# The attention's own-token term as a matrix product through the identity, and a weight subtraction issued half a slot later

## The chip, the cores and the metric

One core of a Trainium2 chip runs the whole program. The metric is the device time of one execution in microseconds (us). The kernel before takes 937.41 us, the median of three runs (937.14 to 937.49).

## The reference

A linear attention with a decaying state, over 4 batches, 8 heads, 768 tokens and 48 channels a head, and then two dense layers with 3072 tokens:

```
for t in range(S):
    cur = einsum('bhd,bhe->bhde', u[None] * k[t], v[t])
    y[t] = einsum('bhd,bhde->bhe', r[t], state + cur)      # cur: the token's own term
    state = w[t][..., None] * state + einsum('bhd,bhe->bhde', k[t], v[t])
x = y as 3072 tokens x 384
x = elu(x @ w_in) @ w_out            # first dense layer, 384 -> 2048 -> 384
x = silu(x @ w_in2) @ w_out2         # second dense layer
```

The token's own term is, for a token and a head, the sum over channels of r*u*k, times the token's value vector v.

## The kernel before, in words

**Units.** The attention is cut into 24 units: 6 stretches of 128 tokens, times 4 batches. For unit n the steps of `prep_steps(n)` run on VectorE (DVE) and ScalarE (ACT): two scans of the decays into the tile `both` (`scan`, `scan_back`), the products r*k (`products`), the scaled r and k (`q`, `kt`, tiles `tq` and `tk`), a range check (`far`, ACT), and for n below SUMMED = 9 the sums of r*u*k for each head on TensorE (PE, `summed`, with u as the moving operand). `diag` then writes, on ACT, the identity matrix times that sum into all eight 128 x 128 blocks of the tile `am` (L201). From unit 9 on GpSimd (POOL) does it in another way (L209). On PE, `pe_steps(n)` makes the scores (`sc`, or `early` for the first four units), DVE copies their strict upper triangle over `am` (`masked`, L312), and `within` multiplies `am` by the values into `y`: 16 matmuls with 32 stationary columns each. So the own term is the diagonal of `am`. `past` (12 such matmuls, L355) adds the state's part, `outer` and `update` renew the state, `split` writes `y` as a rounded part `xh` and the rest `xl`.

**Dense layers.** Tokens go in blocks of four units (512 tokens). A slot is one strip of 128 hidden channels of one block: 9 matmuls into `ph` (`hidden`, L459, three channel groups times the products xh*wh, xl*wh, xh*wl), an activation, a rounding of its result to `gh` (ACT) and `gl` (DVE), and 9 matmuls into `po` for the slot before the last (L490). A block has 16 slots. Here slot s and strip s are numbered from 0, and each of the four units of the next block is spread over the half slots of the present one by `round_ticks`: in block 0 that is units 4 to 7, and the next unit's `prep_steps` run along.

**Weights.** For each strip a load goes to a staging tile `wst` (three buffers, SP queue), ACT scales its halves (`w_scale`, L421, L423), DVE joins them (`w_join`, L430, L432), and `w_split` rounds on ACT (`wh`, L444) and subtracts on DVE (`wl`, L445), whereupon the staging tile is free for the next load. In block 0 the split of strip s+2 is issued in the second half of slot s.

**Order.** The program is recorded under a manual schedule: each engine runs its instructions in the order in which the code issues them, and waits at the head of its own list. `dense_units` writes the order for units 0 to 3, before the first slot; after it come the slots. `behind` is a list of steps that run at the beginning of the next half slot; before, only the last part of `split` goes there.

**Buffers.** `am` has two buffers, `tk` two, `in_w` two. `r*k` (tile `rk`) has a buffer of its own in units 0 to 4 and lies inside `am` after that; `far` writes its unused output into `am`.

Of the kernel before, what the change touches and what calls it, by code (L numbers as in the profile page):

```python
# [34 lines left out]
def kernel(  # L35
# [116 lines left out]
    def prep_steps(n):  # L152
# [32 lines left out]
        def bonus():  # L185
            af = st["af"] = ch_p.tile([128, H * L], F32, tag="am", name="am")
# [7 lines left out]
        def diag(part=0):  # L194
            if n < SUMMED:
                if part == 0:
                    dg = st["dg_sb"] = tok_p.tile([128, H], F32, tag="dg", name="dg")
                    nc.scalar.activation(out=dg, in_=st["dg"], func=ACTF.Copy)
# [4 lines left out]
                return  # L203
            if part:
                return
            dg = tok_p.tile([128, H], F32, tag="dg", name="dg")
            nc.vector.tensor_reduce(
                out=dg, in_=st["kn"].rearrange("p (h d) -> p h d", h=H), axis=mybir.AxisListType.X, op=ALU.add)
            nc.gpsimd.tensor_tensor(  # L209
                out=st["a"].rearrange("p j e t -> p (j e) t"),  # L210
                in0=ident.unsqueeze(1).to_broadcast([128, H, L]),
                in1=dg.unsqueeze(2).to_broadcast([128, H, L]), op=ALU.mult)

        def products():
            if n >= SUMMED:
                return
            if n <= BLOCKS[0]:
                rk = g_p.tile([RB, NP, L], F32, tag="gh", name="rk")
            else:
                rk = st["af"][0:RB, 0:NP * L].rearrange("p (j t) -> p j t", j=NP)  # L220
            st["rk"] = rk
# [24 lines left out]
        def kt():  # L246
            tk = st["kd"] = ch_p.tile([RB, NP, L], F32, tag="tk", name="tk")
# [21 lines left out]
        return dict(ktok=ktok, ktok_copy=ktok_copy, scan=scan, scan_back=scan_back, far=far, whole_decay=whole_decay, bonus=bonus, products=products, summed=summed, diag=diag,  # L269
# [7 lines left out]
    def pe_steps(n, xt, col, free=None):  # L277
# [81 lines left out]
        def within():  # L359
            y = ps["y"]  # L360
            vf = st["v"].rearrange("p j c -> p (j c)")
            for step in range(4):
                for base in range(4):
# [3 lines left out]
                    for kt in range(KT):  # L367
# [8 lines left out]
                        start=not ch and step == 0, stop=step == 3 or todo[step + 1][0] != blk,  # L376
# [59 lines left out]
    def w_split():  # L436
        if whole:
# [7 lines left out]
            nc.vector.tensor_tensor(out=l, in0=t, in1=h.bitcast(F32), op=ALU.subtract)  # L445
# [122 lines left out]
    def round_ticks(n):  # L568
# [9 lines left out]
        def t1():  # L578
# [7 lines left out]
            if n + 1 not in ALONE:  # L586
                load_unit(n + 3, "w")
            pe["masked"](0)

        def t2():  # L590
            pe["masked"](1)
            do("summed")
            do("far")
            do("q")
            do("diag")
# [6 lines left out]
        def t4():  # L602
            do("diag", 1)
            if n < SUMMED - 1:
                do("ktok")
                do("ktok_copy")
# [19 lines left out]
    def dense_units(mask):  # L626
# [19 lines left out]
        for n in range(-1, count):  # L646
# [41 lines left out]
            if more:  # L688
# [5 lines left out]
                p["diag"](0)  # L694
                p["diag"](1)
# [11 lines left out]
        after["kt"]()  # L707
        load_unit(count + 2, "wc")
        after["far"]()
        after["diag"](0)  # L710
        return after
    def prep_rest(at, n, p):

        if n == BLOCKS[0]:
            if at == 1:
                p["diag"](1)
        elif at == 1:
# [5 lines left out]
            load_unit(n + 2, "w")  # L723
        elif at == 2:
# [5 lines left out]
            p["diag"](0)  # L730
            p["diag"](1)
# [42 lines left out]
    with tc.manual_schedule():  # L774
# [11 lines left out]
        first_alone = dense_units(  # L786
# [13 lines left out]
        for j, units in enumerate(BLOCKS):  # L800
# [4 lines left out]
            if ticks and ticks[0] in ALONE:  # L805
                alone = prep_steps(ticks[0]) if j else first_alone

            def tick(part):
# [13 lines left out]
                if j == 0 or final and f % 4 != 3:  # L822
# [19 lines left out]
            assert not todo and not ticks and not behind  # L842
# [195 lines left out]
```

## Time and profile before

| | |
|---|---|
| median of the runs | 937.41 us |
| profiled execution | 938.83 us, of which the span from first to last instruction is 937.1 us |
| PE busy | 919.0 us, 98% of the span |
| DVE, ACT busy | 495.3 us and 501.5 us |
| mean granted PE clock | 0.982 of full speed |

A PE that is busy need not be at its peak, and the granted clock has two levels, 1.2 GHz (shown as 0.50) and 2.4 GHz (1.00). From about 105 us on PE is busy without a pause. Before that it has pauses and stretches at the lower clock, while DVE and ACT are busy most of the time too, and there the three engines wait for each other in turn.

### The profile page before, as it was taken

Reading aid. Unit: us, or ns where it says so; the run is one execution under the profiler, and the core shown is the slowest. Engines: PE = TensorE matmul, PEld = TensorE weight load, DVE = VectorE, ACT = ScalarE, POOL = GpSimd, SP = SyncE. Lnnn points to the kernel's source line nnn. Section 1 sums busy time; section 2 is a strip of 40 time slices with the busy share of each in tenths; the row PEclk is TensorE's granted clock in tenths of the full one; section 3 lists DMA queues with packets and bytes.
Section 4 is the critical chain, followed back from the end, with each engine's and each line's share of the span. In section 5 each row is a group of like instructions: output and inputs, shape, how many; then the busy total and the mean of one; then the engine's idle time right before and its main releaser. Section 6 shows DMA issues by size and latency. Waiting matters only on the chain.

```text
span 937.1 us, 15193 instructions
## 1 busy us (share of the span) xinstructions
PE 919.0 (98%) x6158; PEld 790.0 (84%) x6158; DVE 495.3 (53%) x726; ACT 501.5 (54%) x901; POOL 136.4 (15%) x101
## 2 busy tenths in 40 slices
PE   8899899999999999999999999999999999999997
PEld 7767688888888888888888899999999999899996
DVE  8989988776786776665378852212112222222211
ACT  6798967666555565555488953323333333333322
POOL 0000013463433354442000000000000000000000
PEclk7699999999999999999999999999999999999999
DMA  8655514222221322300245510200200200200001
GB/s 254 156 181 175 167 38 135 67 81 89 82 59 55 102 59 86 97 20 1 102 169 169 176 61 1 68 1 0 69 1 1 68 1 1 68 1 1 34 1 37
DMA packets 32223, 68.69 MB, mean 73 GB/s; under 512 B 3601, under 2 KB 13969, under 8 KB 32145
## 3 DMA queue, kind: packets, MB, share of 16 engines
q1 hardware_dynamic: 32144, 67.64, 23.1%
q8 instruction: 50, 0.82, 0.4%
q14 instruction: 29, 0.23, 0.1%
HBM read 58.19 MB, written 9.44 MB: 72 GB/s over the span
## 4 chain that ended last, share of the span: by engine, by line
PE 91%; DVE 3%; ACT 3%; issue 1%; DVEq 0%
PE ph L459 41%; PE po L498 22%; PE po L490 20%; PE sc L303 2%; PE y L374 2%; PE y L355 2%; ACT am L201 1%; PE ktp L261 1%; PE upd L324 1%; DVE wl L445 1%; DVE am L312 0%; ACT wh L444 0%; PE early L644 0%; DVE wst L430 0%; ACT wst L421 0%
## 5 line engine op out<-in xcount | busy, mean ns | idle before, releaser
L482 DVE TENSOR_TENSOR gl<-g,gh 128x512 fp32r<-128x512 f32 x192 | 146.9, 765 | 317.6 <-ACT gh L481 317.2
L459 PE MATMUL ph<-xh,wl 128*128 128x512 f32 x576 | 227.2, 394 | 2.6 <-DVE wl L445 2.5
L459 PE MATMUL ph<-xh,wh 128*128 128x512 f32 x576 | 227.3, 395 | 1.2 <-ACT wh L444 1.2
L459 PE MATMUL ph<-xl,wh 128*128 128x512 f32 x576 | 226.6, 393 | 0.0
L481 ACT ACTIVATE gh<-g 128x512 fp32r<-128x512 f32 x192 | 120.9, 630 | 145.7 <-PE po L498 109.6
L459 PEld LDWEIGHTS ph<-xh,wl 128*128 128x128 f32 x576 | 108.3, 188 | 28.0 <-DVE wl L445 4.8
L470 ACT ACTIVATE g<-ph 128x512 f32<-128x512 f32 x96 | 57.2, 596 | 138.1 <-PE ph L459 138.1
L498 PE MATMUL po<-wh,gl 128*128 128x384 f32 x384 | 129.5, 337 | 0.0
L498 PE MATMUL po<-wh,gh 128*128 128x384 f32 x384 | 129.3, 337 | 0.0
L498 PE MATMUL po<-wl,gh 128*128 128x384 f32 x384 | 129.0, 336 | 0.0
L459 PEld LDWEIGHTS ph<-xh,wh 128*128 128x128 f32 x576 | 108.5, 188 | 21.7 <-ACT wh L444 1.8
L459 PEld LDWEIGHTS ph<-xl,wh 128*128 128x128 f32 x576 | 108.5, 188 | 19.2
L490 PE MATMUL po<-gh,wh 128*128 128x512 f32 x288 | 114.0, 396 | 0.0
L490 PE MATMUL po<-gl,wh 128*128 128x512 f32 x288 | 112.4, 390 | 0.0
L490 PE MATMUL po<-gh,wl 128*128 128x512 f32 x288 | 112.2, 389 | 0.0
L466 ACT ACTIVATE g<-ph 128x512 f32<-128x512 f32 x96 | 56.8, 592 | 75.7 <-PE ph L459 75.6
L475 DVE SCALAR_TENSOR_TENSOR g<-g,ph 128x512 f32<-128x512 f32 x96 | 65.5, 682 | 43.3 <-ACT g L468 42.3
L498 PEld LDWEIGHTS po<-wh,gh 128*128 128x128 f32 x384 | 72.2, 188 | 4.3
L498 PEld LDWEIGHTS po<-wl,gh 128*128 128x128 f32 x384 | 72.1, 188 | 4.1
L498 PEld LDWEIGHTS po<-wh,gl 128*128 128x128 f32 x384 | 72.0, 188 | 0.0
L237 POOL TENSOR_TENSOR ql<-tq,qh 64x512 fp32r<-64x512 f32 (+1 forms) x30 | 42.6, 1419 | 166.9 <-ACT qh L236 165.8
L490 PEld LDWEIGHTS po<-gh,wh 128*128 128x128 f32 x288 | 54.1, 188 | 11.6 <-issue 0.6
(95 smaller groups left out, 1088.5 us busy)
## 6 DMA issues: line engine op xcount, KB each, us to landing
wst<-in_moe_w_in_dram SPq DMA_DIRECT2D x32, 384.0 KB, 3.3
wst<-in_moe_w_out_dram SPq DMA_DIRECT2D x32, 384.0 KB, 4.4
in_c<-in_rk_ch_dram SPq DMA_DIRECT2D x24, 448.0 KB, 4.3
in_w<-in_w_ch_dram SPq DMA_DIRECT2D x24, 226.2 KB, 2.8
in_v<-in_v_tok_dram SPq DMA_DIRECT2D x24, 224.0 KB, 4.0
x_d<-x2s SPq DMA_DIRECT2D x18, 256.0 KB, 2.5
xl<-x_d SPq DMA_DIRECT2D x6, 768.0 KB, 5.2
out_dram<-os SPq DMA_DIRECT2D x24, 192.0 KB, 2.0
```

Of the source, the lines that this page charges most:

```text
L237: nc.gpsimd.tensor_tensor(out=lo, in0=x, in1=hi.bitcast(F32), op=ALU.subtract)
L303: nc.tensor.matmul(p[:, jj].rearrange("p e t -> p (e t)"), a[:, j, :], b[:, j].rearrange("p e t -> p (e t)"), start=i == 0, stop=i == len( ...
L355: nc.tensor.matmul(y[32 * base:32 * base + 32, kt, :], state[b][:, j, 32 * i:32 * i + 32], st["q"][:, j, :], start=kt == 0, stop=False, sk ...
L374: nc.tensor.matmul(y[32 * base:32 * base + 32, blk // 4, :], vf[:, c:c + 32], st["a"][:, h // 2, h % 2, :], start=not ch and step == 0, st ...
L459: nc.tensor.matmul(ph, lhs, xt[rhs][:, kt, 0:nt], start=n == 0, stop=n == 3 * KT - 1)
L466: nc.scalar.activation(out=g, in_=ph, func=ACTF.Exp)
L470: nc.scalar.activation(out=g, in_=ph, func=ACTF.Silu)
L475: nc.vector.scalar_tensor_tensor(out=g, in0=g, scalar=-1.0, in1=ph, op0=ALU.mult, op1=ALU.max)
L481: nc.scalar.activation(out=gh, in_=g, func=ACTF.Copy)
L482: nc.vector.tensor_tensor(out=gl, in0=g, in1=gh.bitcast(F32), op=ALU.subtract)
L490: nc.tensor.matmul(po[ot][:, 0:nt], lhs, rhs, start=f == 0 and i == 0, stop=f == NF - 1 and i == 2)
L498: nc.tensor.matmul(po[t][:, 0:DM], lhs[:, sl], rhs["o", f], start=f == 0 and i == 0, stop=f == NF - 1 and i == 2)
```

## The change

Five things, all of them for units 0 to 8:

1. `am` is no longer filled with scaled identities. Two fixed tiles `am0`, `am1` are cleared once by POOL; `masked` writes the strict upper triangle, and the rest stays zero.
2. The own term is made by `within`: a tile `vs` holds each token's values times its sum, and 12 matmuls with `vs` stationary and the identity moving add it to `y`, ahead of the 16. `vs` (128 x 384, one buffer) is written by eight ACT operations of 48 columns in units 0 to 4, and by one DVE product in units 5 to 8, one half slot later than before for these.
3. The sums are copied from PSUM by a step of their own, `diag_sums`, ahead of `diag`.
4. `rk` and `tk` are one tile: `kt` overwrites the products in place. `far` writes its unused output into `in_w`, and so the loads of `in_w` stand behind `far`.
5. In block 0 the subtraction `wl` and the next weight load go to `behind`: they are issued at the beginning of the next half slot, behind `gl` of the slot in between.

```diff
+    ams = [one_p.tile([128, H * L], F32, name=f"am{i}") for i in range(2)]
-        for s in state:
+        for s in (*ams, *state):
             nc.gpsimd.memset(s, 0.0)
...
-            to = st["af"][0:RB, 0 if n < SUMMED else H * D:].bitcast(BF16)[:, 0:2 * W1 - 1]
+            to = st["w"].bitcast(BF16)[:, 0:2 * W1 - 1]
...
-                for h in range(part * 4, part * 4 + 4):
-                    nc.scalar.activation(
-                        out=st["a"][:, h // 2, h % 2, :], in_=ident, func=ACTF.Copy, scale=dg[:, h:h + 1])
+                if n > BLOCKS[0]:
+                    nc.vector.tensor_tensor(
+                        out=vs, in0=dg.rearrange("p (j e) -> p j e", e=2).unsqueeze(3).to_broadcast([128, NP, 2, D]),
+                        in1=v3, op=ALU.mult)
+                    return
+                for h in range(H):
+                    nc.scalar.activation(
+                        out=vs[:, h // 2, h % 2, :], in_=v3[:, h // 2, h % 2, :], func=ACTF.Copy, scale=dg[:, h:h + 1])
...
+            rk = st["rk"] = st["kd"] = ch_p.tile([RB, NP, L], F32, tag="tk", name="tk")
             nc.vector.tensor_tensor(out=rk, in0=st["c"][:, 0], in1=st["c"][:, 1], op=ALU.mult)
...
+            if own:
+                vs = st["vs"].rearrange("p j e c -> p (j e c)")
+                for blk in range(KT * 4):
+                    kt, base = divmod(blk, 4)
+                    nc.tensor.matmul(
+                        y[32 * base:32 * base + 32, kt, :], vs[:, 32 * blk:32 * blk + 32], ident,
+                        start=not ch and kt == 0, stop=False, skip_group_check=True)
...
-            nc.vector.tensor_tensor(out=l, in0=t, in1=h.bitcast(F32), op=ALU.subtract)
+            low(lambda: nc.vector.tensor_tensor(out=l, in0=t, in1=h.bitcast(F32), op=ALU.subtract))
...
-                if j == 0 or final and f % 4 != 3:
+                if j == 0 and part:
+                    w_split(behind.append)
+                    behind.append(w_load)
+                elif j == 0 or final and f % 4 != 3:
                     w_tick(part)
```

On PE, among the units before the first slot, unit 0's `within` stands between the transposes of unit 1 (`ktp`) and the sums of unit 2 (`early<-u_ch`). Before:

```order
L295 MATMUL early<-tq,tk 128x128 x8
L261 MATMUL ktp<-ident,tk 128x112 x4
L374 MATMUL y<-am,in_v 32x128 x16
L233 MATMUL early<-u_ch,rk 128x2 x4
L324 MATMUL upd<-in_v,kt 32x48 x3
```

The same place now; the sums read `tk`, which holds the products until `kt` writes it:

```order
L304 MATMUL early<-tq,tk 128x128 x8
L270 MATMUL ktp<-ident,tk 128x112 x4
L376 MATMUL y<-ident,vs 32x128 x12
L391 MATMUL y<-am_101,in_v 32x128 x16
L240 MATMUL early<-u_ch,tk 128x2 x4
L333 MATMUL upd<-in_v,kt 32x48 x3
```

Twelve matmuls came in ahead of the 16, and so ahead of the sums of unit 2.

On DVE, in the same place, unit 2's `tk` (the second row from L248) stands ahead of the first weight join and of unit 1's `masked`; the semaphores that each row waits for stand behind it. Before:

```order
L336 TENSOR_TENSOR packed_105<-upd,whole 112x192 [waits PE_49]
L170 SCALAR_TENSOR_TENSOR both<-in_w,seed 112x515 [waits DVE_49]
L241 TENSOR_TENSOR tq<-in_c,both 112x512
L248 TENSOR_TENSOR tk<-in_c,both 112x512 [waits DVE_49]
L430 SCALAR_TENSOR_TENSOR wst<-wst 128x768 [waits DMAHW4_49,DMAHW3_49,Activation_49]
```

The same place now:

```order
L345 TENSOR_TENSOR packed_107<-upd,whole 112x192 [waits PE_49]
L172 SCALAR_TENSOR_TENSOR both<-in_w,seed 112x515 [waits DVE_49]
L248 TENSOR_TENSOR tq<-in_c,both 112x512
L257 TENSOR_TENSOR tk<-in_c,both 112x512 [waits DVE_49,PE_49]
L447 SCALAR_TENSOR_TENSOR wst<-wst 128x768 [waits DMAHW4_49,DMAHW3_49,Activation_49]
```

The order is the same, and `tk` now waits for PE too: for the sums that read the products in the same tile.

On DVE in block 0, around unit 6's `masked` (L312, now L321) and the `wl` that slot 9 needs. Before:

```order
L170 SCALAR_TENSOR_TENSOR both<-in_w,seed 112x515
L312 COPY_PREDICATED am<-upper,sc 128x4x128
L445 TENSOR_TENSOR wl_0_1128<-wst,wh_0_1127 128x768
L482 TENSOR_TENSOR gl<-g,gh 128x512
L312 COPY_PREDICATED am<-upper,sc 128x4x128
```

The same place now:

```order
L172 SCALAR_TENSOR_TENSOR both<-in_w,seed 112x515
L321 COPY_PREDICATED am_101<-upper,sc 128x4x128
L499 TENSOR_TENSOR gl<-g,gh 128x512
L462 TENSOR_TENSOR wl_0_1183<-wst,wh_0_1182 128x768
L321 COPY_PREDICATED am_101<-upper,sc 128x4x128
```

`gl` and `wl` have changed places, as in every slot of block 0; in two slots before this one a DVE product `vs` was added as well.

## Rows read from the trace of the kernel before

**Rows 1.** The page: busy us, share of the span, instructions of each engine.
```profile
PE 919.0 (98%) x6158; PEld 790.0 (84%) x6158; DVE 495.3 (53%) x726; ACT 501.5 (54%) x901; POOL 136.4 (15%) x101
```
**Rows 2.** Three stretches: PE, PEld, DVE, ACT, POOL busy us, PE clock, DMA share, GB/s.
```profile
0.00:43.00 43.00, 37.13 (x425) 32.46 (x426) 36.78 (x65) 30.88 (x78) 1.74 (x9) 0.68 0.79 224
43.00:97.40 54.40, 48.85 (x408) 36.82 (x407) 48.67 (x73) 48.59 (x96) 0.00 (x0) 1.00 0.47 153
105.00:136.00 31.00, 31.00 (x227) 25.01 (x226) 25.22 (x36) 24.24 (x41) 4.06 (x4) 1.00 0.34 115
```
**Rows 3.** Waits from 43 to 105 us: us, times, longest.
```profile
DVE wl L445 <- ACT wh L444: 5.0, 4, 1.7
...
PE ph L459 <- DVE wl L445: 2.5, 3, 2.0
...
PE ph L459 <- ACT wh L444: 1.2, 2, 0.8
...
PE upd L324 <- DVE am L312: 1.0, 1, 1.0
```
**Rows 4.** PE in order of time: start, us, instruction, idle before and its releaser.
```profile
16.70 1.94 PE L374 MATMUL y<-am,in_v 128*32 128x128 f32 x32
18.57 1.87 PE L233 MATMUL early<-u_ch,rk 112*128 112x2 f32 x8
...
49.62 1.05 PE L233 MATMUL sums<-u_ch,am 112*128 112x2 f32 x8 [0.68 <-DVE am L312]
...
95.05 0.40 PE L459 MATMUL ph<-xl,wh 128*128 128x512 f32 x1
97.40 0.50 PE L459 MATMUL ph<-xh,wl 128*128 128x512 f32 x1 [1.96 <-DVE wl L445]
...
119.45 0.86 PE L355 MATMUL y<-tq,state 112*32 112x128 f32 x24
120.13 0.53 PE L324 MATMUL upd<-in_v,kt 128*32 128x48 f32 x32
```
**Rows 5.** PE clock, in windows of 1 and 0.5 us; columns as in rows 2.
```profile
16.00:17.00 1.00, 1.00 (x12) 0.70 (x15) 1.00 (x3) 1.00 (x3) 0.00 (x0) 0.50 1.03 391
25.00:26.00 1.00, 1.00 (x20) 0.55 (x12) 1.00 (x3) 0.97 (x5) 0.00 (x0) 0.50 0.62 135
97.50:98.00 0.50, 0.50 (x2) 0.46 (x3) 0.50 (x2) 0.50 (x2) 0.00 (x0) 0.77 0.00 0
101.00:101.50 0.50, 0.50 (x28) 0.48 (x22) 0.50 (x2) 0.43 (x1) 0.00 (x0) 0.82 0.96 335
```
**Rows 6.** DVE in order of time, columns as in rows 4.
```profile
19.09 0.68 DVE L248 TENSOR_TENSOR tk<-in_c,both 112x512 f32<-112x512 f32 x1
...
42.92 0.69 DVE L222 TENSOR_TENSOR am<-in_c 112x512 f32<-112x512 f32 x1 [0.95 <-DMA in_c<-in_rk_ch_dram]
...
48.87 0.70 DVE L312 COPY_PREDICATED am<-upper,sc 128x512 f32<-128x512 int8 x1
50.60 0.96 DVE L445 TENSOR_TENSOR wl<-wst,wh 128x768 fp32r<-128x768 f32 x1 [1.03 <-ACT wh L444]
...
88.43 0.96 DVE L445 TENSOR_TENSOR wl<-wst,wh 128x768 fp32r<-128x768 f32 x1 [1.68 <-ACT wh L444]
...
96.41 0.94 DVE L445 TENSOR_TENSOR wl<-wst,wh 128x768 fp32r<-128x768 f32 x1
97.27 0.68 DVE L482 TENSOR_TENSOR gl<-g,gh 128x512 fp32r<-128x512 f32 x1
```
**Rows 7.** ACT in order of time, columns as in rows 4.
```profile
83.61 1.27 ACT L201 ACTIVATE am<-ident,dg 128x128 f32<-128x128 f32 x4
...
88.30 0.62 ACT L481 ACTIVATE gh<-g 128x512 fp32r<-128x512 f32 x1
```
**Rows 8.** Groups to 410 us by form: busy us, mean ns, idle before.
```profile
L390 DVE TENSOR_TENSOR xl<-y,xh 128x384 fp32r<-128x384 f32 x21 | 11.5, 546 | 0.4 <-ACT xh L387 0.3
...
L198 ACT ACTIVATE dg<-early 128x8 f32<-128x8 f32 x5 | 0.8, 169 | 0.4 <-PE early L644 0.4
```

More of the change, by code (lines that the diff above doesn't have):

```diff
@@ L192, in bonus, with diag_sums, diag @@
             nc.gpsimd.tensor_tensor(out=kn, in0=kn, in1=st["r"], op=ALU.mult)
-        def diag(part=0):
+        def diag_sums():
+            dg = st["dg_sb"] = tok_p.tile([128, H], F32, tag="dg", name="dg")
+            nc.scalar.activation(out=dg, in_=st["dg"], func=ACTF.Copy)
+        def diag():
             if n < SUMMED:
-                if part == 0:
-                    dg = st["dg_sb"] = tok_p.tile([128, H], F32, tag="dg", name="dg")
-                    nc.scalar.activation(out=dg, in_=st["dg"], func=ACTF.Copy)
+                vs = st["vs"] = tok_p.tile([128, NP, 2, D], F32, tag="vs", name="vs", bufs=1)
+                v = st["v"]
+                v3 = bass.AP(v.tensor, v.offset, [v.ap[0], (64 + D, NP), (64, 2), (1, D)])
                 dg = st["dg_sb"]
-                for h in range(part * 4, part * 4 + 4):
+                if n > BLOCKS[0]:
[4 more added lines that the diff above has]
+                for h in range(H):
                     nc.scalar.activation(
-                        out=st["a"][:, h // 2, h % 2, :], in_=ident, func=ACTF.Copy, scale=dg[:, h:h + 1])
-                return
-            if part:
+                        out=vs[:, h // 2, h % 2, :], in_=v3[:, h // 2, h % 2, :], func=ACTF.Copy, scale=dg[:, h:h + 1])
                 return
@@ L246, in kt @@
         def kt():
-            tk = st["kd"] = ch_p.tile([RB, NP, L], F32, tag="tk", name="tk")
+            if n >= SUMMED:
+                st["kd"] = ch_p.tile([RB, NP, L], F32, tag="tk", name="tk")
+            tk = st["kd"]
             nc.vector.tensor_tensor(out=tk, in0=st["c"][:, 1], in1=k_decay, op=ALU.mult)
@@ L267, in ktok_copy @@
             nc.scalar.activation(out=t, in_=st["ktp"], func=ACTF.Copy)
-        return dict(ktok=ktok, ktok_copy=ktok_copy, scan=scan, scan_back=scan_back, far=far, whole_decay=whole_decay, bonus=bonus, products=products, summed=summed, diag=diag,
+        return dict(ktok=ktok, ktok_copy=ktok_copy, scan=scan, scan_back=scan_back, far=far, whole_decay=whole_decay, bonus=bonus, products=products, summed=summed, diag=diag, diag_sums=diag_sums,
                     q=q, kt=kt)
@@ L361, in within @@
             vf = st["v"].rearrange("p j c -> p (j c)")
+            own = "vs" in st
+            if own:
[5 more added lines that the diff above has]
+                        start=not ch and kt == 0, stop=False, skip_group_check=True)
             for step in range(4):
@@ L375, in within @@
                         y[32 * base:32 * base + 32, blk // 4, :], vf[:, c:c + 32], st["a"][:, h // 2, h % 2, :],
-                        start=not ch and step == 0, stop=step == 3 or todo[step + 1][0] != blk,
+                        start=not ch and step == 0 and not own, stop=step == 3 or todo[step + 1][0] != blk,
                         skip_group_check=True)
@@ L434, in w_join, with w_split @@
             whole.append((m, f, st[:, :, 1].bitcast(F32)))
-    def w_split():
+    def w_split(low=lambda step: step()):
         if whole:
@@ L585, in t1 @@
             do("whole_decay")
-            if n + 1 not in ALONE:
-                load_unit(n + 3, "w")
             pe["masked"](0)
@@ L593, in t2 @@
             do("far")
+            if n + 1 not in ALONE:
+                load_unit(n + 3, "w")
             do("q")
-            do("diag")
+            do("diag" if n + 1 >= SUMMED else "diag_sums")
         def t3():
@@ L602, in t4 @@
         def t4():
-            do("diag", 1)
             if n < SUMMED - 1:
+                do("diag")
                 do("ktok")
@@ L693, in dense_units @@
                 p["ktok_copy"]()
-                p["diag"](0)
-                p["diag"](1)
+                p["diag_sums"]()
+                p["diag"]()
             if n == -1:
@@ L707, in dense_units @@
         after["kt"]()
+        after["far"]()
         load_unit(count + 2, "wc")
-        after["far"]()
-        after["diag"](0)
-        return after
+        after["diag_sums"]()
+        after["diag"]()
     def prep_rest(at, n, p):
[L714 to L717, printed above, removed]
+        if at == 1:
             p["bonus"]()
@@ L729, in prep_rest @@
             p["far"]()
-            p["diag"](0)
-            p["diag"](1)
+            load_unit(n + 2, "w")
+            p["diag_sums"]()
+            p["diag"]()
     pend, po = [], {}
@@ L785 @@
         setup()
-        first_alone = dense_units(
+        dense_units(
             lambda: nc.scalar.activation(out=upper, in_=above_sb, func=ACTF.Copy))
@@ L805 @@
             if ticks and ticks[0] in ALONE:
-                alone = prep_steps(ticks[0]) if j else first_alone
+                alone = prep_steps(ticks[0]) if j else None
             def tick(part):
@@ L841 @@
                         split_x2(0, f - 11)
-            assert not todo and not ticks and not behind
+            while behind:
+                behind.pop(0)()
+            assert not todo and not ticks
             if j == 0:
```

8 lines of the change are left out of this document (1 added, 7 removed).

## The prediction

> **What bounds the kernel now.** I read the page's engine line first: PE is busy for 919.0 of 937.1 us [rows 1], so nothing but PE's pauses, PE's clock and PE's own work can move the time. Then the stretches: from 105 us PE has no pause at full clock, and any matmul added there costs its whole time; before 43 us PE ran at a mean clock of 0.68; from 43 to 97.4 us it is busy for only 48.85 of 54.40 us, with DVE and ACT at 48.6 us each, three engines nearly full [rows 2]. Then the waits of that stretch: PE waits for the rounded weights (2.5 us for `wl`, 1.2 for `wh`) and once for `masked` (1.0), and DVE waits four times, 5.0 us together, for ACT's `wh` [rows 3]. The last of PE's waits decides: at 95.45 us (the end of the row at 95.05) PE has all but the `wl` of slot 9, gets it at 97.40 [rows 4], and has the lower clock, 1.2 GHz, from within 97.5 to 98.0 until within 101.0 to 101.5 us [rows 5]: by the mixed windows 0.77 and 0.82 from about 97.73 to 101.18, 3.45 us, in which half the work, 1.7 us, was lost. After that PE never waits in block 0. So the time is: when that matmul can run, the clock it runs at, and the PE work behind it.
>
> **The change, part by part.**
>
> *Twelve matmuls more in each of units 0 to 8.* Their nearest row is `past`, also twelve matmuls with 32 stationary columns, and 128 moving: at 2.4 GHz it takes 119.45 to 120.13, 0.7 us. At 1.2 GHz, the 16 of `within` take 16.70 to 18.57, so twelve take 1.4 us [rows 4]. Units 6, 7 and 8 run theirs behind the matmul of 97.40 us, where nothing hides them: 3 x 0.7 = +2.1 us on the path. Units 4 and 5 have theirs before it: 1.4 us of PE that the wait there can cover. Units 0 to 3 have theirs before the first slot, where PE is not full.
>
> *`kt` in place.* DVE's `tk` of unit 2 starts at 19.09 [rows 6]. It now waits for the sums of unit 2 on PE, which end at 18.57 + 1.87 = 20.44, and with unit 0's twelve matmuls ahead of them 1.4 later, at 21.84 [rows 4]. DVE stands for 2.75 us, and behind `tk` in its list stand the weight joins, unit 1's `masked` and everything after. The bounds: 0.3 us if PE were at full clock there (16.70 + 0.7 + 1.0 + 1.05 = 19.4, halving `within`'s 1.94), 2.75 at the lower one; PE is at 0.50 at 16 and still at 25 us [rows 5], so I take 2.75. For unit 3 the sums come 9 us later and are no later than the scan that `tk` needs anyway; in block 0 `tk` follows its sums by several us. DVE has no reserve to make the 2.75 us up: what it then waits for, the load of unit 5's `in_c` (0.95 us at 42.92, [rows 6]), stands on SP behind a weight load that waits for a `wl`, and so moves with it. Unit 5's product starts at 42.92 + 2.75 = 45.67.
>
> *ACT's identities.* In block 0 ACT loses 32 operations, in sets of four of 1.27 us [rows 7]; before block 0, eight of 128 columns become eight of 48, between 0.17 (128x8, [rows 8]) and 0.32 us each (1.27/4), say 0.25, in place of 0.32. One engine's time saved counts only where somebody waits for ACT: the 5.0 us of DVE.
>
> *`vs` on DVE and `wl` behind `gl`.* A DVE `vs` lies between 0.55 us (128x384, [rows 8]) and 0.69 (112x512, [rows 6]); I take 0.55, the same size. Two stand before the deciding `wl`: +1.1 us. That `wl` now has a `gl` ahead of it, 0.68 us [rows 6]. And DVE now waits in each slot for `gh` first, 0.62 us behind `wh` on ACT [rows 7]. Each of the four waits (1.03 us ahead of 50.60 the first, 1.68 ahead of 88.43 the last, [rows 6]) had a set of four identities before it on ACT, as the last has that of 83.61, so each changes by +0.62 - 1.27, and two, which have a `vs` ahead of them on DVE, by -0.55 more: 5.0 - 4 x 0.65 - 1.1 = 1.3 us stay. Between 0 and 5.0 all is possible.
>
> *Small things.* POOL clears two more tiles while it is otherwise idle (1.74 us of 43 busy, [rows 2]), long before `masked` of unit 0. The loads of `in_w` behind `far` are issued about a us later, for a scan that comes a unit later. I count both at nothing; if the cover failed, a scan would wait for a load, and 1 us more would stand on DVE's path.
>
> **The sum.** DVE from unit 5's product to the deciding `wl`: before, 96.41 + 0.94 - 42.92 = 54.4 us, of which 5.0 waiting. Now 49.4 + 1.1 + 0.7 + 1.3 = 52.5, from 45.67: 98.2 us, against 97.40 (+0.8). PE before it: `sums` of unit 5 starts when `masked` has released its bank, 49.62 + 2.75 = 52.4; from there to the deciding matmul it took 95.45 - 49.62 = 45.8 us, of which 0.5 + 1.2 + 1.0 waiting [rows 3, 4] (the 2.5 less the 1.96 itself); 43.1 + 1.4 for units 4 and 5 gives 96.9. PE has a pause ahead of the sums that grows from 0.68 us by up to 2.75. If the clock falls there, 1.7 us more: 98.6. So the matmul runs at 98.2 to 98.6, with a wait of 0 to 1.3 us in place of 1.96, too short to expect the lower clock behind it. Against the profiled execution's 938.83 us (the span of 937.1 and 1.7 around it): +0.8 to +1.2, -1.7 for the clock, +2.1 for units 6 to 8: +1.2 to +1.6, so 940.2 with its overhead. That execution lies 1.4 us above the median of the runs, 937.41; against the median the same sum gives 938.6 to 939.0. I predict 938.7.
>
> **The rivals.**
>
> *PE's clock falls behind the deciding wait as before.* For it: up to 1.3 us of pause may stay. Against: at pauses of 0.7 and 1.0 us earlier [rows 3, 4] the clock held [rows 2]. Then nothing of the 1.7 us comes back: 937.4 + 0.8 + 2.1 = 940.3.
>
> *DVE keeps waiting for ACT (slower).* The mechanism: `gl` at the head of DVE's list waits for `gh`, the last of three ACT operations in the half slot, and holds `wl` behind it. If the whole 5.0 us stay, `wl` ends at 101.9, the clock falls, and the time is 937.4 + 4.5 + 2.1 = 944.0; with half of the difference, 942. It is slower from the point where more than about 1.8 us stay (939.3). For it: each `wl` now has one more ACT result to wait for. Against: ACT has 1.27 us less in every slot with a wait.
>
> *The wait of `tk` does not come, and the change gains.* The Trainium skill, "TensorE: Matmul & The Clock Gate", section "What's actually happening", says that the array is throttled by default and that sustained activity releases it; more matmuls early would then bring 2.4 GHz sooner. This trace does not agree for that stretch: PE is busy for the whole of 16 to 17 and 25 to 26 us at 0.50 [rows 5]. In rows: with full clock from 16.7 us the sums end at 19.4, DVE keeps its times, `wl` ends at 42.92 + 52.5 = 95.4 and PE arrives at 49.62 + 43.1 + 1.4 = 94.1. Then 937.4 - 2.0 - 1.7 + 2.1 = 935.8, and 934.5 if DVE's last 1.3 us of waits go too.
>
> **How the numbers follow.** The forecast (a short wait or none, and the clock holds) has 0.45, with its own range 937.3 to 940; the clock falling again 0.20; DVE waiting on ACT 0.14; no wait of `tk`, or one that DVE makes up, 0.21. What a measurement of this kernel can tell from no change is 0.2%, 1.9 us: 935.5 to 939.3. Faster is most of the last case, 0.17. Slower takes the clock case, the DVE case and the upper end of the forecast: 0.34. Within 0.2% is the rest, 0.49. The range goes from the last case's 935.3 to half way into the DVE case, 941.6.
>
> **What would show each step.** In the profile after: a wait of DVE `tk` for PE of 2 to 3 us at about 19 us; unit 5's product at 45 to 46.5 us; the twelve matmuls at 0.65 to 0.75 us a unit in block 0; DVE waiting for `gh` for 1 to 2 us in all from 45 to 98 us; PE's last wait for a `wl` at about 98 us, under 1.5 us, with the clock at 1.00 behind it; PE without a pause after that. I am wrong if PE's pauses in block 0 vanish altogether, if the deciding `wl` is not that of slot 9, or if the clock in the first 43 us is another.

## The result and the profile after

The changed kernel takes 942.96 us (median; 942.31 to 946.66) against 938.70 us for the kernel before in the same set: 1.0057 times, 95% interval 1.0048 to 1.0067. It is slower, by more than the predicted range. Run once more beside the experiments it gave 941.88 against 937.75 us, 1.0054 (1.0041 to 1.0067).

The page of the changed kernel, its profiled execution (942.39 us, span 940.4 us), in the columns of [rows 1]:

```profile
PE 921.4 (98%) x6374; PEld 794.2 (84%) x6374; DVE 497.8 (53%) x730; ACT 491.2 (52%) x869; POOL 137.7 (15%) x103
```

PE has 2.4 us more work than before, ACT 10.3 us less, and the span is 3.3 us longer. The three stretches that answer to [rows 2], the middle one up to the deciding `wl`:

```profile
0.00:43.00 43.00, 36.60 (x505) 32.64 (x505) 34.67 (x60) 26.70 (x73) 3.52 (x11) 0.72 0.76 221
43.00:99.02 56.02, 50.79 (x474) 39.95 (x471) 52.43 (x80) 46.84 (x86) 0.00 (x0) 1.00 0.47 151
105.00:136.00 31.00, 30.68 (x245) 24.50 (x244) 26.02 (x38) 23.75 (x38) 3.12 (x4) 1.00 0.40 128
```

In the middle ACT is no longer as full as DVE: DVE is busy for 52.43 of 56.02 us and sets the pace. And from 105 us on PE, which had no pause there, has one of 0.32 us. The waits from 43 to 105 us, against [rows 3]:

```profile
ACT wh L461 <- DVE wst L449: 7.8, 7, 2.0
...
PE ph L476 <- DVE wl L462: 4.4, 3, 2.2
...
DVE xl L407 <- ACT xh L404: 2.6, 1, 2.6
DVE gl L499 <- ACT gh L498: 2.4, 5, 0.9
...
PE sums L240 <- ACT kt L276: 0.9, 1, 0.9
```

PE's waits for `wh` and for `masked` are gone, those for `wl` have grown from 2.5 to 4.4 us (2.7 in the second trace, e8, in which the one in slot 2 is absent and PE waits 3.3 us for unit 5's sums instead). DVE no longer waits for `wh`, but five times for `gh`, and ACT now waits for DVE for 7.8 us. PE in order of time, against [rows 4]:

```profile
17.01 1.51 PE L376 MATMUL y<-ident,vs 128*32 128x128 f32 x24
18.29 1.39 PE L391 MATMUL y<-am,in_v 128*32 128x128 f32 x32
19.61 1.05 PE L240 MATMUL early<-u_ch,tk 112*128 112x2 f32 x8
...
54.66 0.50 PE L476 MATMUL ph<-xh,wl 128*128 128x512 f32 x1 [1.37 <-DVE wl L462]
...
85.68 0.50 PE L476 MATMUL ph<-xh,wl 128*128 128x512 f32 x1 [0.79 <-DVE wl L462]
...
96.44 0.39 PE L476 MATMUL ph<-xl,wh 128*128 128x512 f32 x1
99.02 0.50 PE L476 MATMUL ph<-xh,wl 128*128 128x512 f32 x1 [2.19 <-DVE wl L462]
...
101.85 0.84 PE L376 MATMUL y<-ident,vs 128*32 128x128 f32 x24
102.51 1.06 PE L391 MATMUL y<-am,in_v 128*32 128x128 f32 x32
...
132.11 0.50 PE L476 MATMUL ph<-xh,wl 128*128 128x512 f32 x1 [0.32 <-DVE wl L462]
```

In this trace four `wl` come late, in slots 2, 7, 9 and 15; slot 9's is still the longest. The twelve new matmuls take 0.66 us at full clock (101.85 to 102.51). DVE, against [rows 6]:

```profile
20.70 0.69 DVE L257 TENSOR_TENSOR tk<-in_c,both 112x512 f32<-112x512 f32 x1 [1.25 <-PE early L240]
...
43.62 0.56 DVE L407 TENSOR_TENSOR xl<-y,xh 128x384 fp32r<-128x384 f32 x1 [2.56 <-ACT xh L404]
...
45.56 0.69 DVE L229 TENSOR_TENSOR tk<-in_c 112x512 f32<-112x512 f32 x1
...
89.45 0.69 DVE L499 TENSOR_TENSOR gl<-g,gh 128x512 fp32r<-128x512 f32 x1 [0.89 <-ACT gh L498]
...
97.42 0.68 DVE L499 TENSOR_TENSOR gl<-g,gh 128x512 fp32r<-128x512 f32 x1
98.02 0.95 DVE L462 TENSOR_TENSOR wl<-wst,wh 128x768 fp32r<-128x768 f32 x1
```

`tk` waits for PE's sums, unit 5's product starts at 45.56 us, and the deciding `wl` ends at 98.97, right behind a `gl`. PE's clock, in the columns of [rows 5]:

```profile
16.00:17.00 1.00, 1.00 (x6) 0.66 (x4) 1.00 (x2) 0.46 (x1) 0.00 (x0) 0.50 1.08 416
...
19.00:20.00 1.00, 1.00 (x28) 0.80 (x20) 0.45 (x1) 1.00 (x6) 0.00 (x0) 1.00 1.14 330
26.00:27.00 1.00, 1.00 (x25) 1.00 (x21) 1.00 (x1) 0.97 (x5) 0.00 (x0) 0.50 0.35 46
...
99.50:100.50 1.00, 1.00 (x6) 0.80 (x5) 1.00 (x3) 0.57 (x1) 0.00 (x0) 1.00 0.38 61
```

The clock rose at 19 us (before: at 26), fell again, and held behind the wait of 2.19 us.

To compare many traces I use five marks on ACT: the starts of `gh` number 0, 8, 9, 15 and 24, counted from the first of block 0. Number 0 closes the part ahead of the slots; between 8 and 9 lies the stretch behind the deciding `wl`; 15 to 24 holds unit 8. Behind number 24 a kernel's last `gh` follows within 744.9 to 745.3 us in all of the traces below (the fixed `am` tiles and the new place of `far`'s output hold for all 24 units, not for 0 to 8 alone, and nothing of them shows there). Stretches in us ("exchange" is `wl` behind `gl`):

| kernel | to 0 | 0 to 8 | 8 to 9 | 9 to 15 | 15 to 24 |
|---|---|---|---|---|---|
| before | 50.45 | 51.46 | 6.83 | 25.37 | 47.12 |
| before, second trace (e9) | 49.10 | 52.64 | 6.77 | 25.48 | 47.13 |
| after | 52.40 | 50.55 | 6.12 | 27.03 | 47.83 |
| after, second trace (e8) | 51.64 | 51.45 | 5.63 | 27.23 | 47.83 |
| e4: before, with the exchange | 50.14 | 52.48 | 7.37 | 27.04 | 47.13 |
| e10: before, products in place | 51.57 | 51.43 | 6.83 | 25.34 | 47.17 |
| e1: after, no exchange | 52.54 | 49.95 | 5.63 | 26.29 | 47.83 |
| e14: exchange in slots 0 to 6 only | 52.52 | 51.25 | 5.64 | 26.31 | 47.84 |
| e15: exchange from slot 8 on only | 51.28 | 49.52 | 5.64 | 27.05 | 47.84 |
| e12: best | 49.83 | 52.69 | 5.63 | 24.60 | 47.12 |

After minus before is +1.95, -0.91, -0.71, +1.66, +0.71, and +0.6 from number 24 to the span's end, 3.3 us together. Two executions of one kernel differ by up to 1.4 us in the first two columns and by 0.2 in the last two, so small effects ahead of 100 us need the timed ratios.

The marks on ACT follow PE at a varying distance: number 8 starts 4.5 us behind the deciding matmul before and 3.9 us after. What happens behind that matmul is read better from PE's own starts, from the deciding matmul to unit 6's `within`, and on to those of units 7 and 8:

| kernel | deciding matmul at | to unit 6 | 6 to 7 | 7 to 8 |
|---|---|---|---|---|
| before | 97.40 | 4.37 | 18.70 | 31.84 |
| before, second trace (e9) | 97.23 | 4.42 | 18.71 | 31.83 |
| after | 99.02 | 3.49 | 19.38 | 33.06 |
| after, second trace (e8) | 99.15 | 3.49 | 19.37 | 32.79 |
| e1: after, no exchange | 97.91 | 3.51 | 19.39 | 32.45 |
| e4: before, with the exchange | 98.72 | 2.82 | 20.59 | 33.11 |

Before, the first of these stretches ends at

```profile
101.77 1.05 PE L374 MATMUL y<-am,in_v 128*32 128x128 f32 x32
```

Without a new matmul in it that stretch takes 4.4 us where the clock fell (before, e9) and 2.8 us where it held (e4): the fall costs 1.5 to 1.6 us. Each set of twelve matmuls adds 0.6 to 0.7 us (e1 against e4 or before). The exchange adds 0.3 to 0.6 us between units 7 and 8 in the changed kernel (after and e8 against e1), and in e4, on the kernel before, 3.2 us from unit 6 to unit 8.

### The profile page after: what moved, and what is told of

The parts are those of the page before. It is cut to its first block, busy times and chain, and to the rows that moved or that the text cites. A ratio compares the mean times of both kernels' runs of the same rounds, so it can differ in the third digit from the quotient of the medians.

```text
span 940.4 us, 15614 instructions
## 1 busy us (share of the span) xinstructions
PE 921.4 (98%) x6374; PEld 794.2 (84%) x6374; DVE 497.8 (53%) x730; ACT 491.2 (52%) x869; POOL 137.7 (15%) x103
## 4 chain that ended last, share of the span: by engine, by line
PE 87%; DVE 4%; ACT 2%; issue 1%; ACTq 0%
PE ph L476 40%; PE po L515 21%; PE po L507 19%; PE sc L312 2%; PE y L391 2%; PE y L364 1%; DVE wl L462 1%; DVE wst L447 1%; DVE wst L449 1%; ACT wh L461 1%; PE ktp L270 1%; ACT gh L498 1%; PE upd L333 0%; DVE gl L499 0%; DVE am L321 0%
```

## The experiments

Ratios are to the kernel before in the same set, with the 95% interval; 0.001 is 0.94 us. **The theory (A)**: the exchange of `wl` and `gl` costs most, the products in place and the matmuls cost the rest, and the relief of ACT pays part of it back. **The rival (B)** differs from run to run.

**e1_wl_at_once**, the changed kernel without the exchange:

```diff
-                if j == 0 and part:
-                    w_split(behind.append)
-                    behind.append(w_load)
-                elif j == 0 or final and f % 4 != 3:
+                if j == 0 or final and f % 4 != 3:
```

> The changed kernel with one part undone: `wl` and the next weight load are issued at once again, ahead of `gl`. Theory A (DVE's order is what costs: the wl of slot 9 stands behind a gl of 0.6 us, and DVE waits for gh, 0.52 us behind wh, four times between 45 and 98 us, 2.0 us together): that wl ends about 2.2 us earlier, at 96.8 us in place of 98.97, PE's wait there shrinks from 2.19 us to under 0.5, and the wait of 0.32 at 132 us goes; 2.2 to 2.8 us faster than the changed kernel, so a ratio to the kernel before of 1.002 to 1.0035. Theory B (the matmuls added are what costs, 12 in each of units 0 to 8, and DVE's order only moves waits about): within 0.7 us of the changed kernel, a ratio of 1.005 to 1.006.

Measured: 938.96 us, 1.0008 (0.9999 to 1.0017). Against 1.0054 to 1.0057 the exchange costs 4.3 to 4.6 us, more than A said; B falls. (The next weight load moves along with `wl` in this edit; the two were not tried apart. ACT's waits for a load from 45 to 135 us are 0.7 us in the changed kernel's first trace, the line below, and none in its second, which is about as slow, so the later load cannot be much of it.) PE's only wait for a `wl` in block 0:

```profile
97.91 0.50 PE L476 MATMUL ph<-xh,wl 128*128 128x512 f32 x1 [1.04 <-DVE wl L462]
```

DVE's waits for ACT from 45 to 135 us, and ACT's for a load, first of the changed kernel:

```profile
DVE gl L499 <- ACT gh L498: 5.9, 11, 0.9
...
ACT wst L438 <- DMA wst<-in_moe_w_out_dram: 0.7, 3, 0.3
```

and then of this one:

```profile
DVE wl L462 <- ACT wh L461: 3.1, 5, 1.3
...
DVE gl L499 <- ACT gh L498: 0.8, 1, 0.8
```

With the exchange, DVE stands for `gh` in 11 half slots; without it, for `wh` or `gh` in 6, and 2.0 us less. The traces show less than the timed 4.3 to 4.6 us: the deciding matmul runs 1.1 us earlier in e1, and 0.3 to 0.6 us more are gained by unit 8. But e1's profiled execution, 940.94 us, lies 2.0 us above its median.

**e4_defer_only**, the kernel before with the exchange alone:

```diff
+                if j == 0 and part:
+                    w_split(behind.append)
+                    behind.append(w_load)
-                if j == 0 or final and f % 4 != 3:
+                elif j == 0 or final and f % 4 != 3:
```

> The kernel before with one part of the change alone: `wl` and the next weight load at the next half slot's beginning, behind `gl`. Theory A: the wl of slot 9 ends later by the 0.6 us of the gl ahead of it and by up to 0.52 us for each of DVE's four waits, which are now for gh in place of wh: 1 to 2.7 us later, and PE's wait of 1.96 us there grows by as much; 1 to 2.7 us slower than before, a ratio of 1.001 to 1.003. Theory B (the deferral is free, since gl is needed first and wl has a slot's time): a ratio of 0.9995 to 1.0005.

Measured: 941.56 us, 1.0034 (1.0021 to 1.0048), +3.2 us. B falls. PE's waits for `wl` in its first 150 us, and the longest:

```profile
PE ph L459 <- DVE wl L445: 6.9, 5, 2.6
```

```profile
98.72 0.50 PE L459 MATMUL ph<-xh,wl 128*128 128x512 f32 x1 [2.55 <-DVE wl L445]
```

Five late `wl` in place of [rows 3]'s three, and 6.9 us in place of 2.5: the exchange makes these waits by itself. By PE's starts it moves the deciding matmul by 1.3 us and costs 3.2 us behind it, and the clock, which held here, gives 1.5 back.

**e2_rk_apart**, the changed kernel with the products of units 0 to 4 in a tile of their own:

```diff
+            if n <= BLOCKS[0]:
+                rk = st["rk"] = g_p.tile([RB, NP, L], F32, tag="gh", name="rk")
+            else:
                 rk = st["rk"] = st["kd"] = ch_p.tile([RB, NP, L], F32, tag="tk", name="tk")
```

> The changed kernel with one part undone: in units 0 to 4 the products rk have a tile of their own again, and kt does not write over them. Theory A: DVE's wait of 1.25 us for PE's sums at 20.7 us goes, and everything on DVE's list is 1.25 us earlier up to the wl of slot 9: unit 5's product at 44.3 in place of 45.56 us; 1.0 to 1.3 us faster than the changed kernel, a ratio to before of 1.0042 to 1.0048. Theory B: before the first slot PE at the lower clock has become the bound (DVE waits 2.56 us for y of unit 3 at 43.6 us), so the wait of tk is hidden anyway: unit 5's product stays at 45.4 to 45.8 us and the ratio at 1.0055 to 1.006.

Measured: 940.26 us, 1.0026 (1.0016 to 1.0036): 2.6 to 2.9 us less than the changed kernel, above A's figure; unit 5's product starts at 43.58 us, earlier still than A's 44.3. Its first `gh` starts at 49.86 us, against 52.40 and 51.64.

**e10_rk_in_place**, the same part alone, in the kernel before:

```diff
-                rk = g_p.tile([RB, NP, L], F32, tag="gh", name="rk")
+                rk = st["kd"] = ch_p.tile([RB, NP, L], F32, tag="tk", name="tk")
```

> The kernel before with one part of the change: in units 0 to 4 kt overwrites the products in their tile. Theory A (DVE's tk waits for PE's sums before the first slot and all behind it moves): the first gh comes 1.3 to 2.5 us later than 50.45, and 0.8 to 2.8 us stay at the end, 1.001 to 1.003. Theory B (DVE makes the wait up in the slots, where it waits for ACT anyway): 0.9995 to 1.0008, whatever the first gh does.

Measured: 939.33 us, 1.0010 (1.0000 to 1.0021), the low end of A, with an interval that reaches into B. DVE:

```profile
20.47 0.69 DVE L250 TENSOR_TENSOR tk<-in_c,both 112x512 f32<-112x512 f32 x1 [1.30 <-PE early L233]
```

The wait is there without any matmul added: 1.30 us, as 20.44 - 19.09 from [rows 4, 6]. The first `gh` comes 1.1 to 2.5 us later.

**e3_no_own**, the changed kernel without the twelve matmuls (its output lacks the own term of units 0 to 8):

```diff
-            own = "vs" in st
+            own = False
```

> The changed kernel without the twelve matmuls for the own term in units 0 to 8: the output lacks the token's own term there. All else is as in the changed kernel, vs is still computed. Theory A (three of the nine sets lie on the path, 0.65 us each, and two more are hidden in PE's wait at slot 9; the first four cost DVE its wait of 1.25 us at 20.7): 2.0 from units 6 to 8 and about 1.25 from the first four, 3.2 us faster than the changed kernel, a ratio to before of 1.002 to 1.003, with the wait at slot 9 about as long as now or longer. Theory B (all nine sets lie on the path): 9 x 0.65 to 1.4, 7 to 9 us faster, a ratio under 0.999.

Measured: 938.94 us, 1.0014 (1.0005 to 1.0023): the matmuls are worth 3.8 to 4.0 us. B falls. PE's waits for `wl` are no shorter without them; the longest and the clock behind it:

```profile
98.33 0.79 PE L476 MATMUL ph<-xh,wl 128*128 128x512 f32 x1 [2.19 <-DVE wl L462]
```

```profile
99.50:100.50 1.00, 1.00 (x4) 0.81 (x3) 0.97 (x2) 0.00 (x0) 0.00 (x0) 0.50 0.93 292
```

Here the clock fell behind a wait of 2.19 us, the very length behind which it held in the changed kernel.

**e5_both_undone**, the edits of e1 and e2 together:

> The changed kernel with two of its five parts undone at once: the weight subtraction is issued before the next remainder of g as before, and the products r*k of units 0 to 4 have a tile of their own again. Alone, the first gave 1.0008 and the second 1.0026, against 1.0057 for the whole change: -4.6 us and -2.9 us. Theory A (the waits lie at different places, tk's before the first slot and wl's in it, so the effects add up): 1.0057 - 0.0049 - 0.0031 = 0.998, 935.5 to 936.5 us if before is near 938. Theory B (both act on the same deciding wl of slot 9, so only the larger one counts): 1.000 to 1.001, 938 to 939 us, and a wait for wl of 0.5 to 1 us near 98 us stays.

Measured: 937.57 us, 0.9999 (0.9990 to 1.0008). Between A's 0.998 and B's 1.000 to 1.001, nearer B. Added to this kernel, the exchange costs 0.0027 and the products in place 0.0009, both together 0.0055: some 1.8 us more than the sum, which is about what the intervals of the four ratios together allow. My reading, which no run tests by itself, is that DVE makes up most of a late start while it has waits to spare, and little once the exchange has used these up.

**e6_before_pool_diag**, the kernel before, with the identity of units 5 to 8 scaled by POOL:

```diff
                 dg = st["dg_sb"]
+                if n > BLOCKS[0]:
+                    if part == 0:
+                        nc.gpsimd.tensor_tensor(
+                            out=st["a"].rearrange("p j e t -> p (j e) t"),
+                            in0=ident.unsqueeze(1).to_broadcast([128, H, L]),
+                            in1=dg.unsqueeze(2).to_broadcast([128, H, L]), op=ALU.mult)
+                    return
```

> The kernel before with one edit: for units 5 to 8 the identity times the sums is written by GpSimd in one instruction (as from unit 9 on), not by ACT in eight. No matmul is added and nothing is given to DVE. Theory A (what the change gains it gains by taking work off ACT, in the half slots in which DVE waits for wh): DVE's 5.0 us of waits in block 0 shrink, the deciding wl comes 1 to 2 us earlier, the clock holds or falls later, 0.996 to 0.999. Theory B (ACT's work there is hidden, or GpSimd's instruction of about 2 us slows DVE beside it by as much as it saves): 0.9995 to 1.001, with DVE's wl or masked longer than 0.96 and 0.70 us beside it.

Measured: 938.06 us, 1.0008 (1.0000 to 1.0017). B: relieving ACT in this way gains nothing. The trace shows both halves of it. The relief came: DVE's waits for `wh` from 43 to 105 us, 5.0 us in [rows 3], are

```profile
DVE wl L452 <- ACT wh L451: 1.0, 2, 0.6
```

And it was used up: three DVE instructions beside POOL's take 2.52, 2.60 and 1.75 us instead of 0.96, 0.96 and 0.67, 4.3 us more (see the last section).

**e7_vs_pool**, the kernel of e5 with `vs` of units 5 to 8 on POOL (`nc.vector` to `nc.gpsimd` in that product):

> The changed kernel with the subtraction issued at once, products in a tile of their own in units 0 to 4, and vs of units 5 to 8 written by GpSimd and not by DVE. Theory A (DVE's 0.55 us of vs twice before the deciding wl are on its path): 1.1 us faster than the same kernel with vs on DVE, 0.9985 to 0.9990 of it. Theory B (GpSimd is slower at it and within of unit 5 waits for vs, or DVE is slowed beside it): equal or slower by up to 1 us.

Measured: 938.09 us, 1.0003 (0.9993 to 1.0013). A's gain of 1.1 us isn't there.

**e8_after_again** and **e9_before_again**, both kernels unchanged:

> The changed kernel unchanged, beside the same runs of the kernel before as the three others. Both theories: 1.0048 to 1.0067, as measured at first. Below 1.004 the effects of the parts undone, taken as differences from 1.0057, would be smaller than stated.

> The kernel before, unchanged, as a kernel of its own, for a second profiled execution. Its first one took 938.83 us, 1 us more than the median of the runs beside the experiments (937.75 to 937.84). Theory A (the same order gives the same places): ratio 1.000 within 0.001, the first gh within 0.7 us of 50.45, waits for wl of 0.3 to 0.4 and 1.7 to 2.1 us, and the lower clock behind the last. Theory B (what the first profile showed behind the deciding wl, 3.45 us at the lower clock, happens in some executions only): the same ratio, but no lower clock near 98 us, and then the 1.7 us that the forecast gave back were never there in most of the runs.

Measured: 1.0054 (1.0041 to 1.0067) and 0.9996 (0.9987 to 1.0005). The second trace of before has a wait of 1.95 us for the `wl` of slot 9 and 1.2 GHz from within 98.0 to 98.5 until within 101.5 to 102.0 us, like the first: A, though its first `gh`, at 49.10, is 1.35 us earlier than the first trace's, not within 0.7. But again its profiled execution, 938.91 us, lies 1.3 us above its median, 937.60.

**e11_one_at_once**, the changed kernel, with the exchange undone for slot 9's strip alone (`if j == 0 and part and f != 7:`):

> The changed kernel with the subtraction issued at once for a single strip, that of slot 9, the deciding one; the others stay behind gl. Theory A (only that wl decides): PE's wait for it falls from 2.2 us to 0.8 or 1.0 and the time by 1.2 to 1.6 us, 1.0038 to 1.0044. Theory B (the late wl of every slot move DVE's whole row of work, so that the one in slot 9 is only where it shows): 0 to 0.7 us, 1.0048 to 1.0056.

Measured: 941.76 us, 1.0033 (1.0020 to 1.0046). Inconclusive: the ratio is below A's and just excludes B's, the time is that of the changed kernel, and the wait, which A had at 0.8 or 1.0 us, is still there:

```profile
99.25 0.50 PE L476 MATMUL ph<-xh,wl 128*128 128x512 f32 x1 [1.59 <-DVE wl L462]
```

So three more runs split the exchange by slots, in the changed kernel: only for that strip (**e13_one_behind**, `f == 7`), only ahead of it (**e14_behind_to_6**, `f <= 6`), only behind it (**e15_behind_from_8**, `f >= 8`).

> The changed kernel with the subtraction issued at once in every slot but one: only that of slot 9's strip is left behind gl. All at once gave 1.0008, all behind 1.0054. Theory A (the wl of slot 9 alone decides, and each instruction ahead of it costs its own time): PE's wait there is longer by 0.7 to 1.3 us than with all at once, 1.0015 to 1.0022. Theory B (each exchange delays DVE and ACT a little, the delays add up over the slots, and slot 9 is where they show): 1.0005 to 1.0013.

> The changed kernel with the subtraction behind gl for the strips split in slots 0 to 6, and at once from slot 7 on, so from the deciding one. Theory A (only the wl of slot 9 decides): as with all at once, 1.0005 to 1.0015. Theory B (the delays of the earlier slots add up and stay): 1.002 to 1.004, and PE waits for the wl of slots 2 and 7 as in the changed kernel (0.7 to 1.4 and 0.5 to 0.8 us).

> The changed kernel with the subtraction at once for the strips split in slots 0 to 7, and behind gl from slot 8 on, so after the deciding one. Both theories: little, 1.0005 to 1.0018, the 0.3 us wait of slot 15 at most. A third one (PE's path behind slot 9 has no reserve, and each later wl costs): 1.002 to 1.0035, with waits for wl behind 100 us.

Measured: 1.0018 (1.0009 to 1.0027), 1.0036 (1.0023 to 1.0049) and 1.0025 (1.0015 to 1.0035), from 1.0008 without any exchange. The ratio of e13 is in A's range, though its interval holds B's too; e14's is in B's (of the waits that B named only slot 7's came), e15's in the third theory's. In us: 0.9 for the deciding strip, 2.6 for those ahead of it, 1.6 for those behind it, each by 1.2 to 1.5 us uncertain; 5.1 together against 4.3 to 4.6 for all at once, within the intervals. The split is rough: from e11 the deciding strip would be worth 2.0 to 2.3 us and all the others 2.4. In e14 slot 9's `wl` is issued at once and comes late all the same:

```profile
86.49 0.50 PE L476 MATMUL ph<-xh,wl 128*128 128x512 f32 x1 [0.52 <-DVE wl L462]
99.23 0.50 PE L476 MATMUL ph<-xh,wl 128*128 128x512 f32 x1 [1.57 <-DVE wl L462]
```

In e14 and e1 the first `gh` starts at the same time (52.52 and 52.54 us), and the deciding matmul runs 1.3 us later in e14 (99.23 and 97.91): so much of the deciding wait is delay from earlier slots, which only shows there. In e15 the stretch from `gh` 9 to 15 is 27.05 us, and 26.3 without the exchange, and PE waits once more:

```profile
129.48 0.50 PE L476 MATMUL ph<-xh,wl 128*128 128x512 f32 x1 [0.38 <-DVE wl L462]
```

**e12_own_to_5**: the kernel of e5, with the matmuls in units 0 to 5 only, and in units 6 to 8 POOL's identity:

```diff
+            if 6 <= n < SUMMED:
+                nc.gpsimd.tensor_tensor(
+                    out=st["a"].rearrange("p j e t -> p (j e) t"),
+                    in0=ident.unsqueeze(1).to_broadcast([128, H, L]),
+                    in1=st["dg_sb"].unsqueeze(2).to_broadcast([128, H, L]), op=ALU.mult)
+                return
```

> The changed kernel with the subtraction at once, the products in a tile of their own in units 0 to 4, and the own term by matmuls in units 0 to 5 only; for units 6 to 8 GpSimd writes the identity times the sums into am in one instruction. Against the same kernel with the matmuls in all nine units (0.9999). Theory A (the twelve matmuls of units 6, 7 and 8 lie on PE's path at 0.66 us each): 2.0 us faster, 0.9975 to 0.998. Theory B (GpSimd's instruction slows DVE beside it, or unit 6's within waits for it): 0.9990 to 1.0005.

Measured: 937.19 us against 938.27, 0.9985 (0.9975 to 0.9994). It is the one version that beats both kernels. Against e5 the gain is 1.3 us of A's 2.0, with an interval of 0.1 to 2.5; in the traces the stretches from `gh` 9 to 24 shrink from 74.12 to 71.72 us, more than 3 x 0.66. **e16_own_to_4** (`5 <= n`) goes one unit further:

> The best kernel so far (own term by matmuls in units 0 to 5, by GpSimd's identity in 6 to 8, subtraction at once, products in a tile of their own; 0.9985) with unit 5 given to GpSimd too, so that DVE has no vs at all and PE twelve matmuls less. Theory A (DVE's 0.55 us of vs lies ahead of the deciding wl): 0.5 to 1 us faster, 0.9975 to 0.998. Theory B (GpSimd's am of unit 5 comes later than the matmuls' vs, and masked and within wait): 0.9985 to 1.0005.

Measured: 937.76 us, 0.9996 (0.9987 to 1.0005). A's further gain isn't there.

## Why the prediction was wrong

**The step that failed** is the price of `wl` behind `gl`, in two places: "5.0 - 4 x 0.65 - 1.1 = 1.3 us stay" ahead of the deciding `wl`, and "After that PE never waits in block 0" behind it. The first took the four waits of [rows 3] and made each shorter; in the new order every half slot with a `wl` can wait for `gh`, and ahead of the deciding one DVE waited for 2.0 us (four times; 3.0 us, five times, in the second trace). That `wl` ended at 98.97 us, not 98.2: a small miss. The second is the larger: the exchange moves the `wl` of every slot, and the price behind slot 9 was put at nothing. From 45 to 135 us DVE waits for `gh` in 11 half slots; the strips behind the deciding one cost 1.6 us timed (e15), and 0.3 to 0.6 us on PE by unit 8. In all the exchange costs 4.3 to 4.6 us (e1). I priced it at one place, the one that decided before, at 0.7 us, with a net gain from ACT's relief; at that place it costs 0.9 (e13) to 2.3 us (e11), and the other slots make the rest.

**A second term put at nothing**: the matmuls of units 0 to 5. All nine units cost 3.8 to 4.0 us (e3) where the forecast had 2.1, for units 6 to 8. Those three are right in the trace, 0.6 to 0.7 us a unit on PE; what the first six cost follows only as the difference, and how it arises stays open.

**The sum, term by term**, in the two pairs of traces (after and before; e8 and e9):

| term | forecast | traces |
|---|---|---|
| deciding matmul later | +0.8 to +1.2 | +1.6 and +1.9 |
| clock given back | -1.7 | -1.5 and -1.6 |
| matmuls of units 6 to 8 | +2.1 | +2.0 |
| PE behind slot 9 | 0 | +0.6 and +0.3 |

These come to 2.7 and 2.6 us, and the two spans differ by 3.3 and 2.5 us. The forecast had 1.2 to 1.6.

**The rival that came true** is the slower one: DVE keeps waiting, for `gh` now, with `wl` held behind `gl`; its point of "more than about 1.8 us" was passed. Its 942 to 944 holds the first measured 942.96, and 941.88 lies just below. That the exchange is the largest cost is shown by e1 and e4, and its way through the waits for `gh` by the traces. That the number fits is in part luck: the rival counted on the lower clock behind the wait, and the clock held. With 2.0 to 3.0 us staying and the clock held, its own sum gives 937.4 + 0.8 + 0.7 (to 1.7) - 1.7 + 2.1 = 939.3 to 940.3; what filled the rest is behind slot 9, in units 0 to 5, and in the level of the set (below).

**The rest, step by step.** *Products in place*: unit 5's product, predicted at 45.67, started at 45.56 and 45.03. The hit is partly luck: `tk` waited 1.25 and 1.57 us, not 2.75, as the clock rose earlier, and the rest came as a wait for unit 3's `xh` or a load. "DVE has no reserve" fits the changed kernel, where this part is worth 2.6 to 2.9 us (e2), and not the kernel before, where it costs 0.9 us (e10). *PE's arrival* at the deciding matmul, predicted at 96.9 us: 96.83. *The clock* held behind that wait, as forecast, but not for the reason given: the wait was 2.19 us, not up to 1.3, and behind one of 2.19 us it fell in e3. *ACT's relief* is real: e3, with the exchange, the products in place and `vs` but no new matmul, takes 0.0020 less than e4, the exchange alone, 1.9 us with an interval of 0.4 to 3.4. *The range*: its lower end, 935.3, is called the last case's, but that case was worked out as 935.8 or 934.5; nothing hangs on it.

**Against the median.** The forecast started from 937.41 us, the median of three runs. In the set of the result the kernel before took 938.70, so 1.3 of the 4.3 us between 938.7 and 942.96 are that set's level. Against the kernel before in the same set the change costs 4.1 to 4.3 us, where 1.2 to 1.6 us, worked out from the rows of one execution, were forecast. The profiled executions of after and before differ by 3.6 us in the first pair and 2.6 in the second, the medians by 4.3 and 4.1: so 0.7 to 1.6 us of the miss is in no trace. The two profiled executions of before lie 1.4 us above that median of three (but 0.1 above the 938.70 of eight) and 1.3 above the median beside e9; those of after lie 0.4 to 0.6 below theirs. The clock is a part of it: the slower executions of the kernel before tend to have the lower mean granted clock, and the two profiled ones have 0.982 and 0.979, where the median of e9's twelve is 0.984. What else differs stays open.

**The rival of the early clock.** The first stretch at 1.2 GHz ended between 17.0 and 20.5 us in all twelve traces with the new matmuls in units 0 to 3, and at 17.5, 26, 26.5, 37, 40.5 and 44 us in the six without. The Trainium skill, "TensorE: Matmul & The Clock Gate", section "What's actually happening", has sustained activity release the clock; these traces agree in direction, where I had set one row of before against it. So do the timed executions: the median granted clock over the whole run is 0.986 to 0.988 in the twelve runs with these matmuls, and 0.980 to 0.984 in the six without. It did not bring the first slot earlier (first `gh` at 52.40 and 51.64 us, against 50.45 and 49.10), as the clock fell again at 26 us in the changed kernel, with PE waiting for `xl` just ahead (1.94 us).

## What to carry to other kernels

When two instructions change places on an engine that is nearly full, the price can be paid in every repetition, by whatever the one now ahead waits for, and the place that decides shows much of what was lost ahead of it. So price an exchange over the whole loop, with the releaser of the instruction that goes first. Waits on an engine may also be its reserve: the same late start cost 0.9 us alone (e10) and 2.6 to 2.9 us on top of the exchange (e2), though that difference is hardly larger than the noise, and no run tests the reserve by itself.

## What the runs showed of the hardware that was not expected

**DVE beside POOL.** In e12 POOL scales the identity twice from 70 to 100 us:

```profile
73.25 1.90 POOL L202 TENSOR_TENSOR am<-ident,dg 128x1024 f32<-128x1024 f32 x1 [69.19 <-ACT dg L198]
...
97.12 2.14 POOL L202 TENSOR_TENSOR am<-ident,dg 128x1024 f32<-128x1024 f32 x1 [21.98 <-ACT dg L198]
```

and DVE's instruction beside it takes 2.59 us instead of 0.96, and 1.75 instead of 0.67:

```profile
73.37 2.59 DVE L458 SCALAR_TENSOR_TENSOR wst<-wst 128x768 int32<-128x768 int32 x1
...
98.05 1.75 DVE L257 TENSOR_TENSOR tq<-in_c,both 112x512 f32<-112x512 f32 x1
```

So work moved to the idle POOL took 1.1 to 1.6 us from DVE each time. In e6 this is as much as the relief of ACT brought; for e7 and e16 it may be why they gained nothing, which was not tried apart. The Trainium skill, "GPSIMD Engine Reference", section "Specifications", names contention with DVE instructions that have two inputs in SBUF; both of these do, and the trace agrees.

**The clock and a pause of PE.** Behind slot 9's wait it fell after 1.95 and 1.96 us (before, e9, e10), 2.19 (e3) and 2.53 (e13), and held after 1.88 (e6), 2.19 (after, e8), 2.21 (e2) and 2.55 (e4). The length of that pause alone does not tell; what does stays open.
